# A convolution, Fourier-mix and MLP kernel on one core: another order of the opening, and a small norm product moved from VectorE to GpSimd

## The chip, the core and the metric

The kernel runs on one core of a Trainium2 chip. The core has five engines that run at the same time, each working through its own list of instructions in order: TensorE (matrix products; PE in the profile, with its weight loads listed apart as PEld), VectorE (DVE), ScalarE (ACT), GpSimd (POOL) and SyncE (SP), which here only starts DMA transfers. An instruction starts when those ahead of it on its engine have started or ended and the semaphores that it waits for are set. The metric is the device time of one execution in microseconds (us).

## The reference

Input `x` has 8 batches of 4224 positions and 192 features; `weight_gen` gives 8 heads x 7 taps for every position.

```python
w = exp(weight_gen - max(weight_gen, -1)); w = w / (sum(w, -1) + 1e-9)      # softmax over the 7 taps
x = einsum('bshk,bskhg->bshg', w, x_unf)        # causal 7-tap convolution; each head's taps act on its 24 features
u = x + real(fft(fft(x, axis=1), axis=2))       # mix over positions and over features
un = (u - mean(u)) / sqrt(var(u) + 1e-6)        # norm over the 192 features
out = u + maximum(un @ w_ch1, 0) @ w_ch2        # MLP 192 -> 768 -> 192
```

## The kernel before, in words

**Layout.** The 4224 positions of a batch lie as 128 partitions x 33 rows; the first Fourier transform is split into a 128-point and a 33-point part. Everything past the convolution works in nine groups of a batch: eight of four rows and a ninth of one row (suffix `_8`). So a tile name such as `ph_0_3` belongs to batch 0, group 3.

**Stages of one batch.** `conv` makes the taps (`softmax_taps`, lines 271 to 278: load, max, subtract, exp on ACT, sum, reciprocal) and then, for nine chunks of rows, seven products `u`/`pr` on DVE (line 390) that are added up by GpSimd (line 399). GpSimd then folds rows (`sm`, lines 411 and 413), TensorE does the 128-point transform (`pg`, line 418), ACT and DVE put it together (`gt`, lines 423 to 428), and SP writes it to device memory (`g_d`, lines 431 and 432) and reads it back in another layout (`g`, line 447). `transform` does the 33-point part (`pp`, line 457, copied to `pq` by ACT, line 461). `mix` does the transform over features for a group (`eo`, line 486) and adds it to `u` on DVE (lines 492 to 501). `norm` takes the mean and variance of a group: in the first groups ("quick": batch 0 groups 0 to 2, batch 1 groups 0 and 1) on DVE by its statistics instruction, elsewhere on ACT (`junk`, lines 522 and 526). It takes a square root on ACT and a reciprocal on DVE (line 529), then the bias product, mean x reciprocal, one DVE instruction for each of the four rows (line 531), then `un` on ACT (line 534), splits `un` into two fp16 halves (`hl`: line 538 on ACT, lines 540 and 542 on DVE for quick groups and on GpSimd elsewhere), and has a DMA transpose them to `ht` (line 545). `mlp` does six chunks of the first product (`ph`, line 570, five terms each), the relu (`hh`, line 576 alone on ACT; or line 580 on ACT and line 581 on DVE for the low half), the second product of the group before (`po`, line 597) and the closing sum (`u`, line 604), and the result is written out.

**Two forms of the second product.** For the first `F32_GROUPS` groups of batch 0, `po` is one fp32 product with the weights `w2f`, and the relu is one ACT instruction. From then on it is three fp16 terms (`w2h` and `w2l`), and the relu has the second instruction on DVE. The split of `w2f` into `w2h`/`w2l` (`split_w2`) is queued behind MLP group `SPLIT`. The weights come as 64-bit words and are turned into fp32 on DVE in the opening (`words_to_f32`, by `prep_w1` and `prep_w2`), with two scratch tiles in PSUM that share the three buffers of `ph`.

**What sets the order.** Each stage is a generator. `add(start, end, gen)` gives it a stretch of due times in units of one MLP group, and `run()` always advances the one that is due first. So conv of batch b+1, transform and mix of batch b, and the MLP of batch b-1 are woven into each other. The framework then orders every engine's list with its own model of times; `issue_after` (used by `behind` and `queue`) holds work back behind a named instruction: conv(2) behind the last `gt` of conv(1), later convs behind the last product of the one before. In the opening of batch 0 the mix and norm of groups 0 to 2 come first, with the conversion of the weights between them. All DMA transfers start from SP's list.

Of the kernel before, what the change touches and what calls it, by code (L numbers as in the profile page):

```python
# [31 lines left out]
HELD = 7.0  # L32
SPLIT = 5
PP_AT = 4.4
# [3 lines left out]
DVE_ADDS = {(1, c): 1 for c in range(1, NC)}  # L38
F32_GROUPS = 9

# [47 lines left out]
def tile_dynconv_fnet_mlp(  # L88
# [103 lines left out]

    def words_to_f32(raw, out, nm):

        hi, lo = raw[:, :, 1], raw[:, :, 0]
        v = nc.vector
        a, w = [pst("ph", 3, [P, PW], dt, f"{x}_{nm}") for x, dt in (("pa", I32), ("pw", F32))]
        t = temp(f"t_{nm}", I32)
        v.tensor_scalar(out=a, in0=hi, scalar1=3, scalar2=0x3FFFFFFF,
                        op0=ALU.logical_shift_left, op1=ALU.bitwise_and)  # L200
        v.scalar_tensor_tensor(out=t, in0=hi, scalar=-0x40000000, in1=a, op0=ALU.bitwise_and, op1=ALU.bitwise_or)
        v.tensor_scalar(out=a, in0=hi, scalar1=0x7FF00000, scalar2=None, op0=ALU.bitwise_and)
        v.scalar_tensor_tensor(out=w, in0=a, scalar=float(0x38100000), in1=t.bitcast(F32),
                               op0=ALU.is_ge, op1=ALU.mult)
        v.tensor_scalar(out=t, in0=w.bitcast(I32), scalar1=23, scalar2=23,
                        op0=ALU.logical_shift_right, op1=ALU.logical_shift_left)
        v.tensor_scalar(out=a, in0=lo, scalar1=3, scalar2=None, op0=ALU.logical_shift_right)
        r = t.bitcast(F32)
        v.scalar_tensor_tensor(out=r, in0=a, scalar=2.0 ** -49, in1=r, op0=ALU.mult, op1=ALU.mult)
        last_word.append(v.tensor_tensor(out=out, in0=w, in1=r, op=ALU.add))  # L210
# [21 lines left out]
    def prep_w1(raws):  # L232
# [3 lines left out]
        w = temp("w1f_1", F32)  # L236
        words_to_f32(raws[0], w, "w1_1")
        split_f32(w, hi, lo, s1)
# [4 lines left out]
        for i in range(2):  # L243
            cs_ = slice(i * PW, (i + 1) * PW)
            w = temp(f"w1f_0{i}", F32)
            words_to_f32(raws[1 + i], w, f"w1_0{i}")
            split_f32(w, w1h0[:, cs_], w1l0[:, cs_], s1)

    def prep_w2(i):
        words_to_f32(loaded[1][i], w2_part(i)[0], f"w2_{i}")  # L250

# [8 lines left out]
    def softmax_taps(b, parts):  # L260
# [7 lines left out]
        for lo, hi in parts:  # L268
# [5 lines left out]
                                    in1=m[:, sl].unsqueeze(2).broadcast_to([P, n, K]), op=ALU.subtract)  # L274
            nc.scalar.activation(w_sb[:, sl], w_sb[:, sl], AF.Exp)
            nc.vector.tensor_reduce(out=m[:, sl], in_=w_sb[:, sl], axis=AX.X, op=ALU.add)
            nc.vector.tensor_scalar_add(out=m[:, sl], in0=m[:, sl], scalar1=1e-9)
            nc.vector.reciprocal(out=m[:, sl], in_=m[:, sl])
            yield w_sb, m

    def mirrored(ap, step):
# [3 lines left out]
    def conv(b):  # L285

        g_d = g_ds[b % 2]
        parts = [(0, 5), (29, N2), (5, 29)] if b < 2 else [(0, N2)]
        taps = softmax_taps(b, parts)
        part_iter = iter(parts)  # L290
        pieces = iter(X_PIECES)
# [16 lines left out]
        def need_taps(c):  # L308
            nonlocal w_sb, ws
            while not rows_w.issuperset(rows_of(c)):  # L310
                rows_w.update(range(*next(part_iter)))
                w_sb, ws = next(taps)

# [12 lines left out]
        groups = [(NC, 0), (1, 2), (3, 4), (5, 6), (7,)] if b == 0 else [(c,) for c in range(NC + 1)]  # L326
        gt = None
        for grp in groups:
# [39 lines left out]
            for k in range(K):  # L368
                for c, R, u, wp, pa, wq, pt in chunks:
# [27 lines left out]
                    elif k > 0:  # L397
                        adder = nc.vector if k <= DVE_ADDS.get((b, c), 0) else nc.gpsimd
                        adder.tensor_tensor(out=u, in0=u, in1=pr, op=ALU.add)  # L399
                yield (done + sum(q[1] for q in chunks) * k / K) / N2  # L400
            for c, R, u, wp, pa, _, _ in chunks:
                if pa:
# [101 lines left out]
    def norm(b, g):  # L504
# [24 lines left out]
        nc.vector.reciprocal(out=rs[:, 0, 0:T], in_=rs[:, 0, 0:T])  # L529
        for t in range(T):  # L530
            nc.vector.tensor_scalar(out=rs[:, 1, t:t + 1], in0=st[:, t, 0:1], scalar1=rs[:, 0, t:t + 1],  # L531
                                    scalar2=neg, op0=ALU.mult, op1=ALU.mult)
        for t in range(T):
# [104 lines left out]
    def next_conv(b):  # L638
        yield from behind((last_gt if b == 2 else last_product)[b - 1].ins, conv(b))

# [14 lines left out]
    for at in behind(last_fold[0].ins, behind(lp, conv1)):  # L655
        if at > EARLY / N2:
            break
    queue(lp, (prep_w1, loaded[0]))
    for g in range(QUICK):
        add(0.0, 1.0, behind((last_word if g else last_split)[-1].ins, mix(0, g)))  # L660
        run()
        add(0.0, 1.0, norm(0, g))
        run()
        queue(last_bn[0, g].ins, (prep_w2, g))
    for i in range(QUICK, NH // 2):
# [5 lines left out]
    def late_split():  # L671
        yield 0.0
        with tc.issue_after(last_ph[SPLIT].ins):
            queue(last_product[1].ins, (split_w2, None))
        yield 1.0

    def held_mlp(n):
# [11 lines left out]
    for b in range(B):  # L689
# [6 lines left out]
        for g in range(NG):  # L696
            if b > 0 or g >= QUICK:
                at = t0 - mix_at + step * g
                add(at, at + step, mix(b, g))
                add(max(at + step, t0 + g - 2.0), t0 + g - 1.0, norm(b, g))  # L700
# [38 lines left out]
```

## Time and profile before

| what | value |
|---|---|
| runs | median 1191.4 us of 3 (1191.09 to 1192.69) |
| the profiled execution | 1194.52 us, of which its span from the first to the last instruction is 1192.7 us |
| TensorE busy, with weight loads apart | 1095.0 us (92% of the span) |
| VectorE busy | 1027.1 us (86%) |
| GpSimd busy | 867.8 us (73%) |
| ScalarE busy | 779.2 us (65%) |
| mean granted TensorE clock | 0.963 |

Times in the traces count from the start of the span. A row of a timeline gives the start, the duration, engine, line and operation, output and inputs, the number of merged instructions, and in brackets the idle time of that engine just before, with what ended it. A row of the windows gives each engine's busy time in a stretch, and the granted clock of TensorE as a share of full speed. A row of a group of instructions gives its total busy time, the mean duration of one in ns and the idle time before it. Durations in a group overlap by some 0.1 us where an engine is pipelined, so the pace of back-to-back instructions is a little quicker than their mean.

### The profile page before, as it was taken

The numbers are of one execution on the slowest core, as the hardware profiler recorded it, in microseconds if no ns is written. First come the engines' busy times: TensorE is split into PE (matmuls) and PEld (weight loads), VectorE is DVE, ScalarE is ACT, GpSimd is POOL, SyncE is SP. The second block draws the span as 40 slices with busy tenths as digits, with TensorE's granted clock in tenths as the row PEclk, the third lists the DMA queues.
The fourth block names the chain that finished last, engine by engine and source line by source line (L and its number), as shares of the span: only waits on it lengthen the run. The fifth ranks groups of instructions, "written<-read, shape, count | busy, mean of one in ns | idle before, by whom it ended". The sixth has DMA issues, their size and how long they took to land. (4 is left out here: it accounts for less than half of the span.)

```text
span 1192.7 us, 23723 instructions
## 1 busy us (share of the span) xinstructions
PE 1095.0 (92%) x8382; PEld 827.0 (69%) x8382; DVE 1027.1 (86%) x2041; ACT 779.2 (65%) x2353; POOL 867.8 (73%) x686
## 2 busy tenths in 40 slices
PE   4775599899899979998999999899989999999998
PEld 2444377678667857687677777678667876877677
DVE  7999998789999999899999999799998997367533
ACT  1015695254597598757895789657885799589732
POOL 3869579839896999699978999599958997002100
PEclk9896599999999989999999999899999999999999
DMA  8235233731348144733474247413543124412311
GB/s 305 84 98 163 40 60 109 192 89 47 99 127 206 50 123 102 191 87 88 112 198 110 61 114 208 125 48 110 147 121 92 54 58 102 111 45 71 75 50 44
DMA packets 156504, 128.73 MB, mean 108 GB/s; under 512 B 108571, under 2 KB 133088, under 8 KB 156384
## 3 DMA queue, kind: packets, MB, share of 16 engines
q1 hardware_dynamic: 156384, 127.21, 39.4%
q8 instruction: 66, 1.08, 0.4%
q14 instruction: 54, 0.44, 0.1%
HBM read 61.46 MB, written 39.37 MB: 85 GB/s over the span
## 5 line engine op out<-in xcount | busy, mean ns | idle before, releaser
L399 POOL TENSOR_TENSOR u<-u,pr 128x768 f32<-128x768 f32 (+1 forms) x395 | 655.3, 1679 | 69.5 <-DVE pr L390 62.6
L570 PE MATMUL ph<-ht,w1h 128*128 128x512 f16 (+1 forms) x1296 | 401.2, 366 | 20.1 <-DMA ht<-hl 8.8
L597 PE MATMUL po<-w2h,hh 128*128 128x192 f16 x2772 | 395.1, 247 | 6.4 <-DVE u L604 6.0
L597 PEld LDWEIGHTS <-hh 128*128 128x128 f16 x4158 | 355.0, 98 | 65.6 <-issue 7.8
L390 DVE TENSOR_TENSOR pr<-x_sb,wp 128x768 f32<-128x768 f32 (+1 forms) x420 | 358.0, 878 | 21.3 <-POOL u L399 16.8
L597 PE MATMUL po<-w2l,hh 128*128 128x192 f16 x1386 | 337.1, 247 | 0.0
L581 DVE SCALAR_TENSOR_TENSOR hh<-ph,hh 128x512 f16<-128x512 f32 (+1 forms) x378 | 238.7, 640 | 98.1 <-ACT hh L580 96.8
L570 PE MATMUL ph<-ht,w1l 128*128 128x512 f16 (+1 forms) x864 | 312.6, 365 | 0.0
L580 ACT ACTIVATE hh<-ph 128x512 f16<-128x512 f32 (+1 forms) x378 | 207.8, 555 | 136.6 <-PE ph L570 135.7
L540 POOL TENSOR_TENSOR hl<-un,hl 128x512 f16<-128x512 f32 (+1 forms) x67 | 71.9, 1073 | 175.3 <-ACT hl L538 129.4
L570 PEld LDWEIGHTS <-w1h 128*128 128x128 f16 x1296 | 127.2, 100 | 101.6 <-issue 6.1
L534 ACT ACTIVATE un<-u,rs 128x192 f32<-128x192 f32 x264 | 125.6, 537 | 19.8 <-DVE rs L531 12.2
L570 PEld LDWEIGHTS <-w1l 128*128 128x128 f16 x864 | 85.3, 99 | 73.2 <-issue 22.1
L526 ACT ACTIVATE junk<-u,rs 128x192 f16<-128x192 f32 x244 | 110.4, 453 | 3.5
L522 ACT ACTIVATE junk<-u 128x192 f16<-128x192 f32 x244 | 87.8, 360 | 16.6 <-DVE u L496 12.1
L486 PE MATMUL eo<-cs_sb,pq 97*128 97x97 f32 x544 | 79.8, 282 | 17.8 <-DVE u L496 13.3
L486 PEld LDWEIGHTS eo<-cs_sb,pq 97*128 97x128 f32 x544 | 73.8, 198 | 24.4 <-issue 13.1
L461 ACT COPY pq<-pp 97x204 f32<-97x204 f32 (+1 forms) x96 | 46.4, 483 | 60.3 <-PE pp L457 59.4
L597 PE MATMUL po<-w2f,hh 128*128 128x192 f32 x396 | 74.3, 337 | 3.5 <-DVE u L604 3.5
L597 PEld LDWEIGHTS po<-w2f,hh 128*128 128x128 f32 x396 | 68.3, 197 | 9.2 <-DVE u L604 5.2
L604 DVE SCALAR_TENSOR_TENSOR u<-po,isc,u 128x384 f32<-128x384 f32 (+1 forms) x119 | 68.0, 597 | 7.7 <-PE po L597 7.2
L395 PE MATMUL pa<-pr,ident 128*128 128x384 f32 x140 | 54.6, 540 | 20.5 <-DVE pr L390 17.8
(101 smaller groups left out, 1309.7 us busy)
## 6 DMA issues: line engine op xcount, KB each, us to landing
out_dram<-u SPq DMA_DIRECT2D x64, 384.0 KB
x_sb<-in_x_dram SPq DMA_DIRECT2D x48, 384.0 KB
g<-g_d SPq DMA_DIRECT2D x40, 336.0 KB
x_sb<-in_x_dram SPq DMA_DIRECT2D x8, 864.0 KB
g_d<-gt SPq DMA_DIRECT2D x32, 195.0 KB
g_d<-gt SPq DMA_DIRECT2D x32, 189.0 KB
w<-in_weight_gen_dram SPq DMA_DIRECT2D x6, 924.0 KB
x_sb<-in_x_dram SPq DMA_DIRECT2D x8, 672.0 KB
```

What stands on the lines that cost most here:

```text
L390: last_product[b] = nc.vector.tensor_tensor(out=dst, in0=rows, in1=wk, op=ALU.mult)
L399: adder.tensor_tensor(out=u, in0=u, in1=pr, op=ALU.add)
L486: nc.tensor.matmul(eo[:, e, j, :], lhsT=pq[0:DH, e, r, r:r + P], rhs=cs_sb[:, e, :], start=True, stop=True)
L522: nc.scalar.activation(junk, uv[:, t, :], AF.Identity, accum_out=st[:, t, 0:1])
L526: nc.scalar.activation(junk, uv[:, t, :], AF.Square, bias=rs[:, 2, t:t + 1], accum_out=st[:, t, 1:2])
L534: nc.scalar.activation(un[:, t, :], uv[:, t, :], AF.Identity, bias=rs[:, 1, t:t + 1], scale=rs[:, 0, t:t + 1])
L540: lo_eng.tensor_tensor(out=hl[:, 0:T, 2 * P:3 * P], in0=un[:, 0:T, 0:P], in1=hl[:, 0:T, 0:P], op=ALU.subtract)
L570: last_ph[n] = nc.tensor.matmul(ph[:, 0:T], lhsT=wt[:, cs_], rhs=ht[:, 0:T, blk], start=(i == 0), stop=(i == len(terms) - 1))
L580: nc.scalar.activation(a[:, 0:T], ph[:, 0:T], AF.Relu)
L581: nc.vector.scalar_tensor_tensor(out=l[:, 0:T], in0=ph[:, 0:T], scalar=0.0, in1=a[:, 0:T], op0=ALU.max, op1=ALU.subtract)
L597: nc.tensor.matmul(po[jj][:, s, :], lhsT=hx[:, t], rhs=wx[:, c2, :], start=(c2 == 0 and i == 0), stop=(c2 == NH - 1 and i == nt - 1))
L604: nc.vector.scalar_tensor_tensor(out=lt, in0=po[jj][:, 0:m], scalar=scales[0][:, 1:2] if NG * lb + lg < F32_GROUPS else isc, in1=lt, op0=A ...
```

## The change

1. `SPLIT` goes from 5 to 4 and `F32_GROUPS` from 9 to 7: groups 7 and 8 of batch 0 take the three-term fp16 form.
2. The scratch tiles of `prep_w2` take the two buffers of `po` in place of the three of `ph`.
3. The third part of the taps of batch 1 (rows 5 to 28) is made in two steps: load, max, subtract and exp along with `prep_w1`; sum and reciprocal behind the statistics of group (0, 0).
4. In conv(1), what follows the products of chunk 0 (`sm`, `pg`, `gt`) is held back behind those of the next chunk.
5. In `norm`, outside batch 0 and the quick groups, the four DVE products of line 531 become one GpSimd product of 128x4, of values that exist already.
6. conv(2) is held behind the last product of conv(1) instead of its last `gt`.
7. Mix of batch 0 from group 3 on is held behind the first MLP group, and is due 0.7 later.

```diff
-SPLIT = 5
+SPLIT = 4
-F32_GROUPS = 9
+F32_GROUPS = 7
...
-    def words_to_f32(raw, out, nm):
+    def words_to_f32(raw, out, nm, bank):
...
-        a, w = [pst("ph", 3, [P, PW], dt, f"{x}_{nm}") for x, dt in (("pa", I32), ("pw", F32))]
+        a, w = [pst(*bank, [P, PW], dt, f"{x}_{nm}") for x, dt in (("pa", I32), ("pw", F32))]
...
-        words_to_f32(loaded[1][i], w2_part(i)[0], f"w2_{i}")
+        words_to_f32(loaded[1][i], w2_part(i)[0], f"w2_{i}", ("po", 2))
...
             nc.scalar.activation(w_sb[:, sl], w_sb[:, sl], AF.Exp)
+            yield None
             nc.vector.tensor_reduce(out=m[:, sl], in_=w_sb[:, sl], axis=AX.X, op=ALU.add)
...
+    taps = {}
+
+    def tap_step(b, n):
+
+        t = taps[b]
+        while t["n"] < n:
+            t["n"] += 1
+            t["tiles"] = next(t["gen"]) or t["tiles"]
...
-            for c, R, u, wp, pa, _, _ in chunks:
+            tails += chunks
+            while tails and not (b == 1 and grp[0] == 0):
+                c, R, u, wp, pa, _, _ = tails.pop(0)
...
-        for t in range(T):
-            nc.vector.tensor_scalar(out=rs[:, 1, t:t + 1], in0=st[:, t, 0:1], scalar1=rs[:, 0, t:t + 1],
-                                    scalar2=neg, op0=ALU.mult, op1=ALU.mult)
+        if quick or b == 0:
+            for t in range(T):
+                nc.vector.tensor_scalar(out=rs[:, 1, t:t + 1], in0=st[:, t, 0:1], scalar1=rs[:, 0, t:t + 1],
+                                        scalar2=neg, op0=ALU.mult, op1=ALU.mult)
+        else:
+            nc.gpsimd.tensor_tensor(out=rs[:, 1, 0:T], in0=rs[:, 2, 0:T], in1=rs[:, 0, 0:T], op=ALU.mult)
...
-        yield from behind((last_gt if b == 2 else last_product)[b - 1].ins, conv(b))
+        yield from behind(last_product[b - 1].ins, conv(b))
...
     queue(lp, (prep_w1, loaded[0]))
+    queue(lp, (lambda n: tap_step(1, n), 5))
...
+        if g == 0:
+            queue(last_bn[0, 0].ins, (lambda n: tap_step(1, n), 6))
         queue(last_bn[0, g].ins, (prep_w2, g))
...
+    def late_mix(g):
+        yield from behind(last_ph[0].ins, mix(0, g))
...
-                at = t0 - mix_at + step * g
-                add(at, at + step, mix(b, g))
+                at = t0 - mix_at + step * g + (0.7 if b == 0 else 0)
+                add(at, at + step, late_mix(g) if b == 0 and g >= QUICK else mix(b, g))
```

Since the framework orders the lists anew, the diff does not show where things land. Three places follow. Line numbers of the kernel after are higher by 12 to 17 from `conv` on.

TensorE's list in the opening, before, from the mix products `eo` of batch 0 group 2 to the first MLP product `ph` (an `x4` joins four equal instructions):

```order
L486 MATMUL eo_2_874<-cs_sb,pq 128x97 x4
L486 MATMUL eo_3_925<-cs_sb,pq 128x97 x4
L486 MATMUL eo_4_948<-cs_sb,pq 128x97 x4
L418 MATMUL pg_0_666<-sm_0_663,f_sb 128x192 x2
L486 MATMUL eo_5_1022<-cs_sb,pq 128x97 x4
L570 LDWEIGHTS w1h_81
L570 MATMUL ph_0_0_936<-ht_0_810,w1h_81 128x512
```

The same place in the kernel after:

```order
L500 MATMUL eo_2_869<-cs_sb,pq 128x97 x4
L587 LDWEIGHTS w1h_81
L587 MATMUL ph_0_0_920<-ht_0_802,w1h_81 128x512
...
L500 MATMUL eo_3_930<-cs_sb,pq 128x97 x4
...
L500 MATMUL eo_4_979<-cs_sb,pq 128x97 x4
L432 MATMUL pg_1_1084<-sm_1_1081,f_sb 128x192 x2
```

The first MLP group now stands ahead of the mix of groups 3 and 4: fifteen of its products stand before `eo_3` and the other fifteen before `eo_4`.

GpSimd's list at the same time, from the last fold `sm` of batch 1's chunk 1 into chunk 2 (`u_2`), before:

```order
L411 TENSOR_TENSOR sm_1_1024<-u_1_677 128x2x191
L413 TENSOR_TENSOR sm_1_1024<-u_1_677 128x2
L540 TENSOR_TENSOR hl_3_1082<-un_3_1002,hl_3_1082 128x4x128
L542 TENSOR_TENSOR hl_3_1082<-un_3_1002,hl_3_1082 128x4x64
L540 TENSOR_TENSOR hl_4_1218<-un_4_1136,hl_4_1218 128x4x128
L542 TENSOR_TENSOR hl_4_1218<-un_4_1136,hl_4_1218 128x4x64
L399 TENSOR_TENSOR u_2_1191<-u_2_1191,pr_2_2_1206 128x768
```

And after:

```order
L425 TENSOR_TENSOR sm_1_1081<-u_1_665 128x2x191
L427 TENSOR_TENSOR sm_1_1081<-u_1_665 128x2
L411 TENSOR_TENSOR u_2_1180<-u_2_1180,pr_2_2_1195 128x768
L411 TENSOR_TENSOR u_2_1180<-u_2_1180,pr_2_3_1202 128x768
L411 TENSOR_TENSOR u_2_1180<-u_2_1180,pr_2_4_1223 128x768
L557 TENSOR_TENSOR hl_3_1065<-un_3_989,hl_3_1065 128x4x128
L559 TENSOR_TENSOR hl_3_1065<-un_3_989,hl_3_1065 128x4x64
```

The halves `hl` of batch 0's groups 3 and 4 stood ahead of the first add of chunk 2; now three adds go first, and group 4 comes six rows later still.

VectorE's list from the last product of conv(1) to the first of conv(2), with tile numbers, before:

```order
L390 TENSOR_TENSOR pr_1_8_6_1878<-x_sb_66,wp_1_623 128x192
...
L176 TENSOR_REDUCE mx_w2_1779<-ex_w20_1780 128x1
...
L428 TENSOR_TENSOR gt_1_8_1884<-pg_1_8_1882,up_1_8_1886 128x95
L272 TENSOR_REDUCE wp_2_1900<-w_2_1901 128x264
L182 TENSOR_REDUCE m2_w2_1791<-mr_w2_1792 1x1
L273 TENSOR_TENSOR w_2_1901<-w_2_1901,wp_2_1900 128x1848
...
L390 TENSOR_TENSOR u_2_0_1912<-x_sb_66,wp_2_1900 128x768
```

And after:

```order
L176 TENSOR_REDUCE mx_w2_1627<-ex_w20_1628 128x1
...
L402 TENSOR_TENSOR pr_1_8_6_1878<-x_sb_66,wp_1_623 128x192
...
L272 TENSOR_REDUCE wp_2_1900<-w_2_1901 128x264
...
L273 TENSOR_TENSOR w_2_1901<-w_2_1901,wp_2_1900 128x1848
...
L442 TENSOR_TENSOR gt_1_8_1884<-pg_1_8_1882,up_1_8_1886 128x95
L361 TENSOR_TENSOR wp_2_1900<-w_2_1901,wp_2_1900 128x224
L402 TENSOR_TENSOR u_2_0_1912<-x_sb_66,wp_2_1900 128x768
```

The maxima for the weight split (`mx_w2`) went ahead of the end of conv(1), and the taps of conv(2) (`wp_2`, `w_2`) no longer stand behind the last `gt` of conv(1).

More of the change, by code (lines that the diff above doesn't have):

```diff
@@ L236, in prep_w1 @@
         w = temp("w1f_1", F32)
-        words_to_f32(raws[0], w, "w1_1")
+        words_to_f32(raws[0], w, "w1_1", ("ph", 3))
         split_f32(w, hi, lo, s1)
@@ L245, in prep_w1 @@
             w = temp(f"w1f_0{i}", F32)
-            words_to_f32(raws[1 + i], w, f"w1_0{i}")
+            words_to_f32(raws[1 + i], w, f"w1_0{i}", ("ph", 3))
             split_f32(w, w1h0[:, cs_], w1l0[:, cs_], s1)
     def prep_w2(i):
-        words_to_f32(loaded[1][i], w2_part(i)[0], f"w2_{i}")
+        words_to_f32(loaded[1][i], w2_part(i)[0], f"w2_{i}", ("po", 2))
     def split_w2(_):
@@ L288, in conv @@
         parts = [(0, 5), (29, N2), (5, 29)] if b < 2 else [(0, N2)]
-        taps = softmax_taps(b, parts)
-        part_iter = iter(parts)
+        taps[b] = dict(gen=softmax_taps(b, parts), n=0, tiles=None)
+        part_iter = iter(range(len(parts)))
         pieces = iter(X_PIECES)
@@ L310, in need_taps @@
             while not rows_w.issuperset(rows_of(c)):
-                rows_w.update(range(*next(part_iter)))
-                w_sb, ws = next(taps)
+                i = next(part_iter)
+                rows_w.update(range(*parts[i]))
+                tap_step(b, 2 * i + 2)
+                w_sb, ws = taps[b]["tiles"]
         if b > 0:
@@ L326, in conv @@
         groups = [(NC, 0), (1, 2), (3, 4), (5, 6), (7,)] if b == 0 else [(c,) for c in range(NC + 1)]
-        gt = None
+        gt, tails = None, []
         for grp in groups:
@@ L399, in conv @@
                         adder.tensor_tensor(out=u, in0=u, in1=pr, op=ALU.add)
-                yield (done + sum(q[1] for q in chunks) * k / K) / N2
-            for c, R, u, wp, pa, _, _ in chunks:
+                yield (done + sum(q[1] for q in tails) + sum(q[1] for q in chunks) * k / K) / N2
+            tails += chunks
+            while tails and not (b == 1 and grp[0] == 0):
+                c, R, u, wp, pa, _, _ = tails.pop(0)
                 if pa:
```

## The prediction

> **What bounds the kernel now.** The totals come first:
>
> ```profile
> PE 1095.0 (92%) x8382; PEld 827.0 (69%) x8382; DVE 1027.1 (86%) x2041; ACT 779.2 (65%) x2353; POOL 867.8 (73%) x686
> ```
>
> TensorE is the busiest engine, but 92% is a mean over stages. The chain of waits says what the end hung on:
>
> ```profile
> 888.85 2.80 DMA g_d<-gt
> 891.79 3.57 DMA g<-g_d
> 895.50 2.40 PE pp L457 x16
> ...
> 1188.14 1.66 PE po L597 x18
> ```
>
> The end hangs on `pp` of batch 6 at 895.50, and that on the round trip of `gt` through memory behind conv(6). Next come the windows, each from the first product of one conv to that of the next, conv(1)'s chunk 2 first. The columns are the length, then the busy time of PE, PEld, DVE, ACT and POOL, then PE's clock, DMA share and GB/s:
>
> ```profile
> 152.80:255.40 102.60, 97.26 (x532) 74.52 (x530) 84.22 (x143) 54.10 (x148) 76.46 (x60) 0.97 0.49 126
> 255.40:381.10 125.70, 117.58 (x873) 88.92 (x873) 120.92 (x243) 86.15 (x257) 110.75 (x84) 1.00 0.41 106
> 381.10:506.80 125.70, 116.85 (x972) 88.48 (x971) 120.23 (x242) 96.83 (x300) 112.55 (x88) 0.97 0.45 122
> 506.80:631.90 125.10, 119.77 (x1017) 92.34 (x1015) 118.81 (x240) 95.89 (x299) 112.72 (x88) 0.99 0.46 120
> 631.90:757.80 125.90, 123.60 (x1039) 95.49 (x1038) 121.20 (x244) 98.52 (x303) 113.01 (x88) 0.99 0.44 120
> 757.80:887.40 129.60, 122.96 (x1025) 94.16 (x1023) 121.68 (x244) 96.41 (x298) 110.45 (x84) 0.97 0.41 111
> 887.40:1021.10 133.70, 130.58 (x1090) 100.25 (x1088) 117.07 (x243) 99.01 (x307) 115.16 (x92) 0.99 0.34 87
> 1021.10:1192.70 171.60, 168.14 (x1478) 129.27 (x1476) 83.49 (x186) 102.77 (x308) 14.98 (x18) 1.00 0.23 61
> ```
>
> From 887 on TensorE idles 133.70 - 130.58 + 171.60 - 168.14 = 6.6 us in 305: it alone is the bound. In the five windows from 255.4 to 887.4 DVE idles 4.8, 5.5, 6.3, 4.7 and 7.9 us (29.2 together), TensorE 8.1, 8.9, 5.3, 2.3 and 6.6 (31.2), GpSimd 13 to 19: DVE and TensorE are nearly tied, GpSimd close behind. In the first window nothing but TensorE is full (DVE 82%, POOL 75%), so conv(1) and what follows it take longer than their work. A shift there is handed on from conv to conv, as far as TensorE keeps up.
>
> **The change part by part.** *Before conv(1)'s chunk 2.* Its products came behind the third part of the taps, and GpSimd's adds behind the `hl` of groups 3 and 4:
>
> ```profile
> 142.22 1.55 DVE L272 TENSOR_REDUCE wp<-w 128x192 f32<-128x1344 f32 x1
> ...
> 149.00 1.56 DVE L276 TENSOR_REDUCE wp<-w 128x192 f32<-128x1344 f32 x1 [1.85 <-ACT w L275]
> ...
> 152.82 0.95 DVE L390 TENSOR_TENSOR u<-x_sb,wp 128x768 f32<-128x768 f32 x1
> ```
> ```profile
> 153.30 1.16 POOL L540 TENSOR_TENSOR hl<-un,hl 128x512 f16<-128x512 f32 x1 [16.41 <-ACT hl L538]
> ...
> 159.43 1.16 POOL L540 TENSOR_TENSOR hl<-un,hl 128x512 f16<-128x512 f32 x1 [4.34 <-ACT hl L538]
> ...
> 161.17 5.60 POOL L399 TENSOR_TENSOR u<-u,pr 128x768 f32<-128x768 f32 x3
> ```
>
> The DVE work of the taps is not saved, it moves ahead; the wait of 1.85 us goes, and part of the mix and norm of groups 3 to 5 now falls behind the products. I take -5 us for the first product (bounds -2, the wait alone, and -10.6, all from 142.22 to 152.82). The first add no longer waits for both `hl` (8.35 us behind the first product until now). With five products and one DVE add ahead of it I take it 7 us earlier, at 154.2. From there GpSimd has to work off the adds of conv(1); the two `hl` pairs, some 1.8 us each (159.43 to 161.17), now lie among these, which gives back 3.6. So conv(1) ends some 3.5 us earlier, between 0 and 7.
>
> *From conv(1) to conv(2).*
>
> ```profile
> 229.07 0.35 DVE L390 TENSOR_TENSOR pr<-x_sb,wp 128x192 f32<-128x192 f32 x1 [0.20 <-POOL u L399]
> ...
> 229.87 4.17 DVE L175 TENSOR_SCALAR ex_w<-w2f 128x384 int32<-128x384 int32 x3
> ...
> 242.08 0.26 DVE L427 TENSOR_TENSOR gt<-pg,up 128x95 f32<-128x95 f32 x1 [5.03 <-ACT up L425]
> ...
> 255.39 0.95 DVE L390 TENSOR_TENSOR u<-x_sb,wp 128x768 f32<-128x768 f32 x1
> ```
> ```profile
> 365.59 0.34 DVE L390 TENSOR_TENSOR pr<-x_sb,wp 128x192 f32<-128x192 f32 x1
> ...
> 381.08 0.95 DVE L390 TENSOR_TENSOR u<-x_sb,wp 128x768 f32<-128x768 f32 x1
> ```
>
> From the last product of one conv to the first of the next it is 255.39 - 229.07 = 26.3 us here, and 381.08 - 365.59 = 15.5 one batch on, where the taps don't stand behind the last `gt`. The new list makes this transition like the later ones, and the 4.17 us for the weight split moves into conv(1), where DVE idles 18 us. I take 15 for the 26.3, so -11.5 (bounds -5, the wait of 5.03 alone, and -14). Conv(2) starts 3.5 + 11.5 = **15 us earlier**, at 240.4 (bounds 5 and 21, both ends together).
>
> *Norm's bias product.*
>
> ```profile
> 145.68 0.57 DVE L531 TENSOR_SCALAR rs<-st,rs 128x1 f32<-128x1 f32 x4
> ```
> ```profile
> L531 DVE TENSOR_SCALAR rs<-st,rs 128x1 f32<-128x1 f32 x264 | 38.2, 205 | 0.5
> L581 DVE SCALAR_TENSOR_TENSOR hh<-ph,hh 128x512 f16<-128x512 f32 x336 | 227.5, 684 | 91.1 <-ACT hh L580 89.9
> ```
> ```profile
> L413 POOL TENSOR_TENSOR sm<-u 128x2 f32<-128x2 f32 x64 | 14.8, 231 | 0.0
> ```
>
> Four take 0.57 us. Of 264, batch 0 and batch 1's two quick groups keep 33 + 8 = 41, so 223 go: 33 a batch, 33 x 0.57 / 4 = 4.7 us. GpSimd gets nine products a batch. None like it is in the trace; between the 128x2 fold (0.23) and a pair `hl` (1.8), it is nearest to the fold, so 9 x 0.23 = 2.1 us a batch. If DVE set the pace, each of the five windows would shorten by 4.7; if GpSimd did, it would lengthen by 2.1. Neither does alone: GpSimd adds behind DVE's products within a chunk, DVE sets the transitions, and TensorE idles only 2.3 us in the fourth window.
>
> ```profile
> POOL u L399 <- DVE pr L390: 46.3, 12, 22.8
> ```
> ```profile
> DVE pr L390 <- POOL u L399: 5.8, 11, 1.5
> ```
>
> These waits from 255 to 888 show both directions; without the 22.8 of the first start, GpSimd waits 23.5 us for DVE. I take 0 for the product in the five windows (bounds -4.7 and +2.1 each).
>
> *The fp16 form of groups 7 and 8.*
>
> ```profile
> 170.76 4.17 PE L597 MATMUL po<-w2f,hh 128*128 128x192 f32 x24 [1.45 <-DVE u L604]
> ```
> ```profile
> 1112.84 0.99 PE po L597 x12
> ```
>
> A group of four rows takes 48 fp32 products at 4.17 / 24 = 0.174 us, 8.3 us, or 72 in fp16 at 0.99 / 12 = 0.083, 5.9 us: 2.4 less for group 7, a quarter of it for group 8, 3 us of TensorE. On DVE it adds 6 relu halves of 0.684 and 6 shorter ones, some 5.5 us, and the order puts those of group 7 into conv(2)'s chunk 2. DVE idles 4.8 us in that window, so half is hidden: **+2.5 us** (bounds 0 and 5.5; without cover 5.5).
>
> *TensorE's order.* With the first MLP group ahead of the mix of groups 3 and 4, TensorE has work sooner, but that group runs against ACT, which makes its relus and the norm of group 3; the order of what follows is as before, and I take 0 for TensorE's idle time up to 150 (bounds -4 and +4). Counting the products of the new list at their durations, `pp` of batch 2 has 15.8 us less work ahead of it and that of batch 6 2.2 less, so TensorE has 13.6 us more to do in between.
>
> ```profile
> 383.10 0.91 PE L457 MATMUL pp<-te_sb,g 102*97 102x102 f32 x8 [1.17 <-DMA g<-g_d]
> ```
>
> From 383.10 to 895.50, about the last four of the five windows, it idles 8.9 + 5.3 + 2.3 + 6.6 = 23.1 us. With both `pp` 12.5 us earlier it would have 9.5 left, 2.4 a window, as little as the fourth window has now (2.3): just enough. No term, but a bound for what follows. Behind `pp` of batch 6 there are 290 us of its work in both lists: 0.
>
> **Sum:** -15 + 0 + 2.5 + 0 = -12.5 us. The profiled execution took 1194.52, 3.1 over the median of the runs, so 1182.0 for it, and **1179** for the median.
>
> A row that speaks of a price beside this:
>
> ```profile
> 141.89 0.42 DVE L542 TENSOR_TENSOR hl<-un,hl 128x256 f16<-128x256 f32 x1
> ```
> ```profile
> L542 DVE TENSOR_TENSOR hl<-un,hl 128x256 f16<-128x256 f32 x5 | 7.7, 1542 | 0.0
> ```
>
> The same instruction on DVE took 0.42 us where GpSimd was idle, and 1.54 on average. The Trainium skill, "GPSIMD Engine Reference", section "8. Key points", says that GpSimd shares its SBUF interfaces with VectorE and contends with instructions that have two SBUF inputs; by it, 2.1 us more of GpSimd in a batch cost DVE at most 2.1 x (1 - 0.42 / 1.54) = 1.5 us (an estimate), five times 7.5, if DVE did nothing but such instructions, and the sum would be -5 instead of -12.5. The trace agrees on the direction, but the convolution's product on DVE, the commonest, reads its taps from PSUM.
>
> **The rivals.** *DVE sets the pace, the gain grows.* For it: DVE idles less than TensorE in the first two of the five windows. `pp` of batch 2 would come 15 - 2.5 + 4.7 = 17.2 us earlier. Against it: TensorE has only 23.1 - 13.6 = 9.5 us of idle time to give up from there on, and will keep one a window: 17.2 + 5.5 = 22.7, 1169; with the opening at its bound of 21, 1163.
>
> *GpSimd sets the pace.* Its adds hardly pause within a chunk, and five windows times 2.1 give back 10.5: -15 + 10.5 = -4.5, 1187. Against it: it idles 13 to 19 us in each window.
>
> *TensorE doesn't use the earlier conv(2).* It is busy for 97.26 of 102.60 us in the first window already, and the 13.6 us more behind `pp` of batch 2 may cost it what conv gains; then only the 3 us of saved products remain: 1188.5, at the edge of no change. Against it: that idle time is in part waiting for this very chain, as the 1.17 us at 383.10.
>
> *Slower: GpSimd waits at the new product.* It works in order. The product waits for DVE's reciprocal, and that for ACT's square root; the adds behind it wait too, and DVE's products for their buffers. The price is the wait, up to 1.8 us for the reciprocal where DVE itself waited:
>
> ```profile
> DVE rs L529 <- ACT rs L528: 8.1, 8, 1.8
> ```
>
> Over the 45 products of the five windows it decides from (15 - 10.5 + 2.4) / 45 = 0.15 us each; at 0.4 it is -4.5 + 18 = +13.5, 1205. For it: the old products stood on the engine that also makes the reciprocal, the new one crosses to another. Against it: 8.1 us in 8 waits is little in a whole run.
>
> **How the numbers follow.** A difference under 0.2%, 2.4 us, can't be told from none here. Chances: the forecast, between -20 and -8, 0.50; DVE 0.09; GpSimd 0.17; TensorE 0.13, half of it within 0.2%; slower 0.11. That is 0.825 faster, 0.065 the same, 0.11 slower. The range is 1164 to 1191: below, nearly to the end of DVE's case; above, past GpSimd's and TensorE's, short of the slower one.
>
> **What would show it.** Right: conv(2)'s first product near 240 and `pp` of batch 2 near 371; windows of 125 to 129 us after that; `pp` of batch 6 near 883, and 297 us from there to the end. The wait of 16.41 for `hl` ahead of GpSimd's adds is gone, and the new product takes under 0.3 us. Wrong at the opening: conv(2) starts after 250. Wrong at the product: GpSimd shows a wait for the reciprocal of more than 7 us in all, or adds pause behind it. Wrong on the hand-over: conv(2) is early and `pp` of batch 6 is not; then either DVE's or TensorE's idle time in the windows tells which took it.

## The result, and the profile after

The kernel after takes **1174.94 us** (median of 4 runs, 1171.40 to 1176.11) against 1191.87 for the kernel before in the same session, 16.9 us less by the medians. The ratio of the runs is 0.9845, 95% interval 0.9815 to 0.9874, which makes 18 us, and the two spans that are compared below differ by 18.4. The forecast was 1179, 12.5 us less, in a range of 1164 to 1191. Direction and range were right; the size was a quarter to a third too small, and the experiments show that some of the reasons behind it were wrong.

The totals and TensorE's clock from the page of the kernel after (span 1174.3 us):

```profile
PE 1087.7 (93%) x8412; PEld 823.8 (70%) x8412; DVE 1007.1 (86%) x1830; ACT 774.0 (66%) x2351; POOL 874.7 (74%) x747
```

TensorE is idle 1174.3 - 1087.7 = 86.6 us instead of 97.7. The windows of the kernel after, cut at the same places as before (from conv(1)'s chunk 2, then from the first product of one conv to that of the next; columns: length, busy PE, PEld, DVE, ACT, POOL, PE's clock, DMA share, GB/s):

```profile
145.80:240.90 95.10, 91.58 (x504) 71.38 (x504) 84.86 (x160) 56.48 (x166) 75.40 (x60) 0.98 0.43 120
240.90:369.20 128.30, 116.63 (x862) 88.83 (x861) 120.84 (x224) 86.84 (x260) 111.34 (x91) 0.93 0.42 114
369.20:494.00 124.80, 122.72 (x1043) 94.83 (x1041) 118.77 (x211) 98.68 (x304) 114.07 (x98) 1.00 0.48 123
494.00:619.90 125.90, 123.86 (x1040) 95.15 (x1038) 118.45 (x212) 97.95 (x301) 113.93 (x97) 0.99 0.48 124
619.90:745.90 126.00, 123.51 (x1038) 95.38 (x1037) 117.71 (x211) 97.66 (x302) 114.00 (x97) 0.99 0.45 120
745.90:874.80 128.90, 124.28 (x1058) 95.61 (x1057) 119.12 (x214) 98.07 (x303) 113.84 (x97) 1.00 0.47 117
874.80:1174.30 299.50, 293.82 (x2548) 225.88 (x2546) 190.91 (x360) 198.30 (x610) 130.68 (x124) 1.00 0.28 71
```

And the last stretch of the kernel before, cut in the same way:

```profile
887.40:1192.70 305.30, 298.72 (x2567) 229.52 (x2564) 200.56 (x429) 201.78 (x615) 130.14 (x110) 0.99 0.28 72
```

Conv(2) starts 14.5 us earlier (255.4 to 240.9) and conv(3) 11.9 (381.1 to 369.2). The next four windows add up to 505.6, where they were 506.3. The last stretch, in which TensorE has hardly a pause, is 5.8 us shorter, mostly because TensorE has 293.82 us left to do there instead of 298.72: with windows as long as before it got more done in them (494.4 us busy against 483.2 from conv(3) to conv(7)). So the 18.4 us of the two spans are 11.9 up to conv(3) and 6.5 behind it. TensorE's clock is lower in one window: from conv(2) to conv(3) it was granted 0.93 of full speed, in the kernel before 1.00.

How the opening came about, on VectorE and then on GpSimd (timeline of the kernel after):

```profile
145.79 0.95 DVE L402 TENSOR_TENSOR u<-x_sb,wp 128x768 f32<-128x768 f32 x1
...
226.53 0.34 DVE L402 TENSOR_TENSOR pr<-x_sb,wp 128x192 f32<-128x192 f32 x1
...
227.39 2.08 DVE L272 TENSOR_REDUCE wp<-w 128x264 f32<-128x1848 f32 x1
...
240.94 0.95 DVE L402 TENSOR_TENSOR u<-x_sb,wp 128x768 f32<-128x768 f32 x1
```
```profile
152.34 5.63 POOL L411 TENSOR_TENSOR u<-u,pr 128x768 f32<-128x768 f32 x3 [18.35 <-DVE u L411]
157.93 1.16 POOL L557 TENSOR_TENSOR hl<-un,hl 128x512 f16<-128x512 f32 x1
```

The products of chunk 2 start 7.0 us earlier (152.8 to 145.8), the adds 8.9 (161.2 to 152.3) and without the wait for `hl`; conv(1)'s last product comes 2.5 us earlier (229.1 to 226.5), and the way from there to conv(2) takes 14.4 us instead of 26.3.

### The profile page after: what moved, and what is told of

Same layout as the page of the kernel before. It is cut to its first block, busy times and chain, and to the rows that moved or that the text cites. A ratio compares the mean times of both kernels' runs of the same rounds, so it can differ in the third digit from the quotient of the medians.

```text
span 1174.3 us, 23548 instructions
## 1 busy us (share of the span) xinstructions
PE 1087.7 (93%) x8412; PEld 823.8 (70%) x8412; DVE 1007.1 (86%) x1830; ACT 774.0 (66%) x2351; POOL 874.7 (74%) x747
## 4 chain that ended last, share of the span: by engine, by line
PE 31%; ACT 9%; POOL 7%; issue 6%; DVE 3%; DMA 3%; SPq 0%; POOLq 0%; DVEq 0%; ACTq 0%
PE po L614 13%; PE ph L587 13%; POOL u L411 5%; PE pp L471 3%; ACT un L551 2%; ACT hh L597 2%; DMA g<-g_d 2%; ACT junk L540 2%; PE eo L500 1%; ACT junk L536 1%; DMA g_d<-gt 1%; POOL hl L557 1%; PE pg L432 1%; ACT hl L555 1%; DVE pr L402 1%
## 5 line engine op out<-in xcount | busy, mean ns | idle before, releaser
L614 PE MATMUL po<-w2h,hh 128*128 128x192 f16 x2832 | 408.2, 248 | 8.0 <-DVE hh L598 6.9
L614 PEld LDWEIGHTS <-hh 128*128 128x128 f16 x4248 | 364.7, 99 | 67.4 <-DVE hh L598 7.5
L614 PE MATMUL po<-w2l,hh 128*128 128x192 f16 x1416 | 345.6, 248 | 0.0
L598 DVE SCALAR_TENSOR_TENSOR hh<-ph,hh 128x512 f16<-128x512 f32 (+1 forms) x390 | 244.1, 633 | 112.5 <-ACT hh L597 111.5
L597 ACT ACTIVATE hh<-ph 128x512 f16<-128x512 f32 (+1 forms) x390 | 212.7, 550 | 147.5 <-PE ph L587 146.4
L425 POOL TENSOR_TENSOR sm<-u 128x382 f32<-128x382 f32 x64 | 64.5, 1008 | 7.0 <-ACT u L420 6.8
L614 PE MATMUL po<-w2f,hh 128*128 128x192 f32 x336 | 63.9, 334 | 3.0 <-DVE u L621 3.0
```

The lines of the kernel that those rows point to most:

```text
L597: nc.scalar.activation(a[:, 0:T], ph[:, 0:T], AF.Relu)
L598: nc.vector.scalar_tensor_tensor(out=l[:, 0:T], in0=ph[:, 0:T], scalar=0.0, in1=a[:, 0:T], op0=ALU.max, op1=ALU.subtract)
L614: nc.tensor.matmul(po[jj][:, s, :], lhsT=hx[:, t], rhs=wx[:, c2, :], start=(c2 == 0 and i == 0), stop=(c2 == NH - 1 and i == nt - 1))
```

## The experiments

Every kernel was timed against the kernel before on the same chip. The table has the ratio with its interval, and from the one profiled execution the start of conv(2) and of conv(3), and the time from there to the end of the span.

| kernel | ratio (95% interval) | conv(2) | conv(3) | conv(3) to end |
|---|---|---|---|---|
| before | 1 | 255.4 | 381.1 | 811.6 |
| after | 0.9845 (0.9815 to 0.9874) | 240.9 | 369.2 | 805.1 |
| u_product: after, product on VectorE | 0.9928 (0.9908 to 0.9948) | 241.7 | 371.1 | 814.0 |
| o_product: before, product on GpSimd | 0.9963 (0.9947 to 0.9979) | 254.1 | 381.9 | 803.9 |
| u_last_gt: conv(2) behind the last `gt` | 0.9916 (0.9903 to 0.9930) | 251.2 | 375.8 | 807.1 |
| u_f32: SPLIT 5, F32_GROUPS 9 | 0.9943 (0.9923 to 0.9963) | 239.2 | 379.8 | 803.7 |
| s4_f9: SPLIT 4, F32_GROUPS 9 | 0.9896 (0.9868 to 0.9923) | 241.6 | 375.4 | 805.0 |
| u_taps: taps in one step | 0.9936 (0.9915 to 0.9957) | 245.7 | 381.9 | 804.9 |
| u_mix: mix not held back | 0.9920 (0.9899 to 0.9940) | 247.9 | 383.3 | 807.2 |
| u_bank_tails: scratch in `ph`, tail not held | 0.9901 (0.9882 to 0.9921) | 245.8 | 373.9 | 807.1 |
| x_product0: product on GpSimd in batch 0 too | 0.9892 (0.9863 to 0.9922) | 245.2 | 374.4 | 807.9 |
| s3_f6: SPLIT 3, F32_GROUPS 6 | 0.9926 (0.9909 to 0.9942) | 242.9 | 375.7 | 808.3 |
| l_term: less TensorE work | 0.9827 (0.9812 to 0.9842) | 241.0 | 371.4 | 801.1 |
| d_product: product made four times | 1.0172 (1.0151 to 1.0194) | 241.0 | 369.3 | 842.9 |

The profiled execution of u_mix took 7 us more than the median of its runs and that of u_taps 4 more, the others were within 3.1 of theirs. Executions of one kernel differ by up to 12 us (x_product0: 1174.99 to 1187.35), so a difference of a few us between two rows is not firm. The last two kernels do other work behind conv(3). Of the other twelve, the ten with the product on GpSimd take 803.7 to 808.3 us from conv(3) to the end and the two with it on VectorE 811.6 and 814.0, whatever the opening did. So in these executions nearly every difference between them is made in two places: at the start of conv(3), and by the product.

### The product, there and back

u_product:

```diff
-        if quick or b == 0:
+        if True:
```

> The kernel after with the bias product back on VectorE (four small products a group instead of one on GpSimd). Theory (the gain is made in the opening, and from conv(3) to conv(6) TensorE sets the pace, so the product moves nothing there): within 3 us of the kernel after, 1172 to 1178, conv(2) still starting near 241. Rival (VectorE's relief of 4.7 us a batch is what shortened conv(6) and conv(7), where some 6 us more were gained than forecast): 1179 to 1183, conv(7) taking 110 us from its first to its last product instead of 105.8. Third (the product on GpSimd costs, since it waits for the reciprocal): 1165 to 1171.

o_product is the kernel before with the `else` branch of the change in `norm` and nothing else.

> The kernel before with nothing but the bias product moved to GpSimd. Theory: no change beyond 3 us, 1188 to 1195. Rival (VectorE's relief counts): 1180 to 1187. Third (GpSimd sets the pace, 2 us a batch and waits for the reciprocal): 1196 to 1206.

The theory fell in both, in the second narrowly. u_product's 1185.9 lies above its rival's band of 1179 to 1183 too; by the ratio it would be 1183.3. Taken back, the product costs 0.9928 / 0.9845, some 10 us; put into the kernel before it saves 0.37%, 4.4 us. The windows of u_product from conv(3) on:

```profile
371.10:497.40 126.30, 123.50 (x1045) 94.86 (x1045) 121.20 (x244) 97.96 (x305) 115.22 (x92) 1.00 0.46 122
497.40:621.50 124.10, 119.84 (x1017) 92.61 (x1018) 120.71 (x244) 96.40 (x300) 112.75 (x88) 1.00 0.44 119
621.50:747.50 126.00, 121.15 (x1036) 93.54 (x1034) 120.80 (x243) 98.24 (x300) 112.20 (x86) 1.00 0.47 120
747.50:878.50 131.00, 125.39 (x1026) 95.89 (x1025) 121.32 (x245) 97.42 (x300) 111.02 (x86) 0.96 0.44 118
878.50:1185.10 306.60, 301.26 (x2601) 231.02 (x2599) 202.40 (x431) 201.34 (x617) 130.07 (x110) 1.00 0.28 70
```

Up to conv(7), conv runs at nearly the same pace as in the kernel after (507.4 us against 505.6). Conv(7) itself takes 108.9 us from its first product to the end of its last, where the kernel after takes 105.9 and the rival had said 110; but the ten kernels with the product on GpSimd lie between 105.8 and 108.6 there, so this sign separates little. Behind its last product another 4.1 us are lost (197.8 against 193.7). So the rival had a part of it right, and most of the loss lies behind the start of conv(7). VectorE is busy 2.2 to 3.1 us longer in each window, and TensorE gets 489.9 us done in the four windows instead of 494.4; the stretch from conv(7) on is 7.1 us longer and holds 7.4 us more of TensorE's work. That the MLP falls behind because its relus stand in VectorE's fuller list fits this; the runs don't separate it from other ways.

The product itself, in the kernel after:

```profile
L549 POOL TENSOR_TENSOR rs<-rs 128x4 f32<-128x4 f32 x54 | 10.9, 206 | 64.3 <-DVE rs L543 60.4 <-ACT junk L540 3.9
```

### More of GpSimd, less of TensorE

d_product makes the same product four times; the output does not change:

```diff
-            nc.gpsimd.tensor_tensor(out=rs[:, 1, 0:T], in0=rs[:, 2, 0:T], in1=rs[:, 0, 0:T], op=ALU.mult)
+            for _ in range(4):
+                nc.gpsimd.tensor_tensor(out=rs[:, 1, 0:T], in0=rs[:, 2, 0:T], in1=rs[:, 0, 0:T], op=ALU.mult)
```

> The kernel after with the product on GpSimd made four times instead of once, 0.6 us more of GpSimd a group and 5.4 a batch, with the same output. Theory (GpSimd has slack in the windows, 114 of 125 us): from conv(3) to the end it stays at 804 to 809, ratio 0.984 to 0.989. Rival (within a conv GpSimd sets the pace, with 0.6 to 3 us of idle time there): about 5 us more a batch from conv(3) on, 825 to 830, ratio 1.002 to 1.010.

l_term leaves out one term of the first MLP product in batches 1 to 5, so its output is not the whole result:

```diff
-                terms = ((w1h0, 0), (w1l0, 0), (w1h0, 2), (w1h1, 1), (w1l1, 1))
+                terms = ((w1h0, 0), (w1l0, 0), (w1h0, 2), (w1h1, 1), (w1l1, 1))[:4 if 1 <= b <= 5 else 5]
```

> The kernel after with one of the five terms of the first MLP product (low weights on the last 64 features, w1l1) left out in batches 1 to 5, so that TensorE has some 6 x 0.216 = 1.3 us less to do in a group, 11 in a batch, 53 in all; the other engines do the same work. So far the time from conv(3)'s first product to the end was 804 to 807 in seven kernels with the product on GpSimd and 812 to 814 in two with it on VectorE. Theory (behind conv(3) TensorE, with 17 us of idle time in 804, sets the end, VectorE next to it): the windows of 125 us from conv to conv shorten only to VectorE's work, 119 to 121, but the rest behind conv(7) gets shorter too: ratio 0.945 to 0.965, TensorE's idle time much larger. Rival (TensorE alone): 53 us less, ratio 0.938 to 0.942. Rival (the chain over VectorE and GpSimd sets the windows, and the end hangs on it): windows stay within 1 us of 125, ratio 0.970 to 0.983.

l_term speaks against TensorE as the bound of the windows. With some 42 us less to do (TensorE busy 1045.5 us in place of 1087.7), it is hardly faster than the kernel after: the intervals 0.9812 to 0.9842 and 0.9815 to 0.9874 overlap. Its ratio is at the slow end of the third case, and three of its windows (126.7, 125.9, 130.9 and 126.5 us) are longer than that case said, with TensorE idling 7 to 14 us in each. The four add up to 510.0 us, where the kernel after has 505.6. The first three:

```profile
371.40:498.10 126.70, 118.58 (x1041) 93.64 (x1039) 119.77 (x215) 97.47 (x304) 113.81 (x97) 1.00 0.48 127
498.10:624.00 125.90, 117.82 (x1022) 92.50 (x1021) 119.45 (x213) 98.44 (x305) 114.04 (x97) 0.99 0.46 122
624.00:754.90 130.90, 116.46 (x969) 92.50 (x968) 117.59 (x211) 97.01 (x301) 114.03 (x97) 0.93 0.45 120
```

In the third of them TensorE's clock was 0.93, and over the whole execution 0.954 against 0.965. From conv(7) on less work does show: the last stretch is 291.1 us instead of 299.5, for 15.0 us less of TensorE's work.

d_product is 3.3% slower than the kernel after, some 39 us, for 904.1 - 874.7 = 29.4 us of GpSimd's time. Its windows:

```profile
511.00:639.00 128.00, 122.90 (x1030) 93.56 (x1028) 117.93 (x208) 92.83 (x291) 115.50 (x119) 0.99 0.45 119
639.00:770.60 131.60, 128.78 (x1080) 99.22 (x1078) 118.82 (x213) 101.90 (x309) 117.77 (x124) 0.99 0.46 121
770.60:902.00 131.40, 122.47 (x1021) 94.02 (x1019) 119.25 (x210) 97.15 (x299) 118.00 (x124) 0.99 0.40 104
```

GpSimd has 1.6, 3.8 and 4.2 us more to do in them than in the kernel after, and they are 2.1, 5.6 and 2.5 us longer, in sum about one for one, though GpSimd still idles 12 to 14 us in each. But this does not show that GpSimd sets the pace. The framework did not keep the four products of a group together. In one group of conv(2) the first starts at 318.01 and the fourth at 328.21, and `un`, which reads them, comes behind the fourth; in the kernel after that group's one product is at 317.78 and its `un` at 321.55. So the norm is late by more than the products take:

```profile
318.01 0.20 POOL L550 TENSOR_TENSOR rs<-rs 128x4 f32<-128x4 f32 x1
...
328.21 0.20 POOL L550 TENSOR_TENSOR rs<-rs 128x4 f32<-128x4 f32 x1
329.48 1.85 ACT L552 ACTIVATE un<-u,rs 128x192 f32<-128x192 f32 x4
```

And the window before them (conv(3), 141.7 us) is 16.9 longer, of which GpSimd's own work explains 3.3. There the list of VectorE's waits does not name GpSimd; it waited 15.9 us for the relu on ACT, in the kernel after 0.8. A row of waits gives the total in us, how often, and the longest (this window in d_product, then in the kernel after):

```profile
DVE hh L599 <- ACT hh L598: 15.9, 13, 4.5
```
```profile
DVE hh L598 <- ACT hh L597: 0.8, 3, 0.3
```

The relu in turn waited for TensorE's products, and TensorE had a late start: at 375.39 it had waited 4.66 us for `g`, and the eight products that took 0.91 us in the kernel after (370.64) took 1.65, at a granted clock of 0.62 from 370 to 382:

```profile
375.39 1.65 PE L471 MATMUL pp<-te_sb,g 102*97 102x102 f32 x8 [4.66 <-DMA g<-g_d]
```

What the two show together is less than a bound: TensorE's work does not set the pace of 125 us, and more work for GpSimd in the middle of the norm costs more than its own time. Whether that is GpSimd's share or the later norm, and what then sets the pace, was not settled; each of the two kernels also has a list of its own.

### The opening, part by part

```diff
-        yield from behind(last_product[b - 1].ins, conv(b))
+        yield from behind((last_gt if b == 2 else last_product)[b - 1].ins, conv(b))
```

> The kernel after with conv(2) held behind the last gt of conv(1) again. Theory (the way from conv(1) to conv(2) is worth some 11 us of the 15 at conv(2)'s start, and is handed on to the end): conv(2) starts 5 to 11 us later, at 246 to 252, and the time is 1180 to 1186. Rival (a later start is made up in the next batches by TensorE's idle time): conv(2) later by as much, the time within 3 us of the kernel after.

Here the theory held: conv(2) starts 10.3 us later, and the ratio of 0.9916 against 0.9845 is 8.5 us more.

```diff
-SPLIT = 4
+SPLIT = 5
-F32_GROUPS = 7
+F32_GROUPS = 9
```

> The kernel after with SPLIT 5 and F32_GROUPS 9 again. Theory: 3 us more of TensorE's work, 5.5 less of VectorE's in the first window, and the weight split falls behind conv(1) again (some 5 us of VectorE at the transition): conv(2) starts 3 to 6 us later, the time is 1176 to 1181. Rival (the fp16 form costs VectorE more than it saves TensorE): 1168 to 1173.

s4_f9 has only the second of the two lines.

> The kernel after with F32_GROUPS 9 again but SPLIT left at 4: the two changes of u_f32 taken apart. Theory A (u_f32 lost because the split of the weights fell into the start of conv(2), where VectorE then waited 6.28 us for a product that stands far back on TensorE): the split stays inside conv(1), so only the 3 us of TensorE's work come back: ratio to before 0.985 to 0.989. Theory B (the fp32 form of groups 7 and 8 is what cost): 0.992 to 0.996, as u_f32.

Neither expectation was met, s4_f9's theory A by a hair (0.9896, said up to 0.989). u_f32 starts conv(2) no later but earlier, at 239.2, and loses it all in the window that follows, 140.6 us in place of 128.3, in good part because the split of the weights now stands among the products of conv(2). VectorE's timeline there:

```profile
252.86 0.16 DVE L185 TENSOR_SCALAR m_w<-me_w 128x1 f32<-128x1 f32 x1 [6.28 <-PE me_w L184]
```

A tiny instruction waits 6.28 us for TensorE, and the products behind it wait too. s4_f9 keeps the split inside conv(1) and gets back half (0.9943 to 0.9896). The other half, 0.9896 against 0.9845 or 6 us, is left to the fp32 form of groups 7 and 8, though the two intervals touch (0.9868 to 0.9923 and 0.9815 to 0.9874). Its window of conv(2) is 133.8 us, and TensorE's timeline there shows one long wait for a closing sum on VectorE:

```profile
285.80 7.20 PE L614 MATMUL po<-w2f,hh 128*128 128x192 f32 x26 [7.92 <-DVE u L621]
```

The 26 products behind it take 0.277 us each where 24 of the same took 0.174 in the kernel before (170.76), at a clock of 0.67 from 277.7 to 293 instead of 1.00. So with F32_GROUPS at 7 this kernel is some 6 us faster, where the forecast had a cost of 2.5; how much of that is the form and how much the place of one wait in the list isn't separated.

u_taps takes out the two queued steps, so that the third part of the taps is made ahead of chunk 2 again; u_mix makes `late_mix` and the 0.7 void:

```diff
-    queue(lp, (lambda n: tap_step(1, n), 5))
...
-        if g == 0:
-            queue(last_bn[0, 0].ins, (lambda n: tap_step(1, n), 6))
```
```diff
-                at = t0 - mix_at + step * g + (0.7 if b == 0 else 0)
-                add(at, at + step, late_mix(g) if b == 0 and g >= QUICK else mix(b, g))
+                at = t0 - mix_at + step * g
+                add(at, at + step, mix(b, g))
```

> The kernel after with the third part of batch 1's taps again made right ahead of the products of conv(1)'s chunk 2. Theory: the first product of chunk 2 comes some 5 us later than in the kernel after (145.8), at 149 to 153, conv(2) by 2 to 5 later, ratio to before 0.987 to 0.991. Rival (VectorE works the same amount by then and the wait of 1.85 us is hidden anyway): within 2 us of the kernel after, 0.983 to 0.986.

> The kernel after with mix of batch 0 from group 3 on neither held behind the first MLP group nor due 0.7 later. Theory: the first MLP products fall behind the mix of groups 3 to 5 again and the mix takes VectorE ahead of conv(1)'s chunk 2: that starts 4 to 7 us later than at 145.8, ratio 0.988 to 0.993. Rival (the taps alone make the earlier start): within 2 us, 0.983 to 0.986.

The start of chunk 2 came as expected, at 151.6 and 150.4, and conv(2) 4.8 and 7.0 us later. u_mix met its expectation with 0.9920; u_taps lost 11 us, more than the expected band. Both then wait in the window of conv(2) for the relu of an MLP group that isn't far enough (VectorE's timeline of u_taps, then of u_mix):

```profile
266.53 0.69 DVE L598 SCALAR_TENSOR_TENSOR hh<-ph,hh 128x512 f16<-128x512 f32 x1 [6.70 <-ACT hh L597]
```
```profile
268.02 0.69 DVE L598 SCALAR_TENSOR_TENSOR hh<-ph,hh 128x512 f16<-128x512 f32 x1 [4.28 <-ACT hh L597]
```

u_bank_tails:

```diff
-        words_to_f32(loaded[1][i], w2_part(i)[0], f"w2_{i}", ("po", 2))
+        words_to_f32(loaded[1][i], w2_part(i)[0], f"w2_{i}", ("ph", 3))
...
-            while tails and not (b == 1 and grp[0] == 0):
+            while tails:
```

> The kernel after with the scratch tiles of prep_w2 in the three buffers of ph again, and the tail of conv(1)'s chunk 0 not held back. Theory: the first MLP group waits for a scratch tile again, as before (4.1 us at its third chunk), while the end is set later: ratio 0.985 to 0.988. Rival (TensorE's idle time counts in full wherever it lies): 0.988 to 0.991.

It came out in the rival's band, 0.9901, 7 us slower, but conv(2) also started 4.9 us later, so this is no proof of the rival. Both edits show as waits of TensorE in the opening: 15.09 us for the fold of conv(1) ahead of `pg` at 128.15, and 6.05 and 5.54 us for VectorE's work on the weights ahead of the first MLP products at 135.86 and 143.69. Which of the two sets the later conv(2) was not tried.

The six undos cost 10, 8.5, 12, 11, 9 and 7 us, 57 together, three times what the change brings. They are not parts of a sum: each gets its own list, and a part that loses a few us at conv(2) can meet a wait behind it that the full change does not have. A rival stands untested here: the kernel after may have a list that happens to fit, so that any edit costs some us whatever it does. All nine edits of it that keep the whole computation and its work (the six undos, s4_f9 and the two below) are slower, by 6 to 12 us, in whichever direction they go, and no edit that should change nothing was run beside them. The product stands on firmer ground, since it also gained 4.4 us in the kernel before.

### Further in the same direction

x_product0 drops `or b == 0` from the condition in `norm`; s3_f6 has SPLIT 3 and F32_GROUPS 6.

> The kernel after with the product on GpSimd in batch 0's groups 3 to 8 too, 21 small VectorE products less in the opening, 3 us. Theory (the opening hangs on VectorE up to conv(2), and what conv(3) gains is handed on): ratio 0.981 to 0.984. Rival (GpSimd is the fuller engine in conv(1), the product waits there for the reciprocal): 0.986 to 0.992.

> The kernel after with SPLIT 3 and F32_GROUPS 6, one step further in the direction of the change: the split of the weights is queued a group earlier and group 6 takes the fp16 form, 2.4 us less of TensorE, 4.1 more of VectorE. Theory (conv(2) starts where it does, and TensorE's saving shows at conv(3)): ratio 0.981 to 0.985. Rival (VectorE's extra work in the opening costs as much or more): 0.986 to 0.990.

Both are slower than the kernel after, by 6 and 10 us, x_product0 within its rival's band (its interval touches that of the kernel after), s3_f6 beyond its own. In x_product0 GpSimd waits at the first of the new products, between the start of conv(1)'s chunk 2 at 146.8 and conv(2)'s at 245.2 (waits of GpSimd there):

```profile
POOL rs L549 <- DVE rs L543: 17.5, 1, 17.5
POOL u L411 <- DVE pr L402: 1.5, 2, 0.9
```

This wait takes the place of one that GpSimd had there anyway (18.35 us at 152.34, above). What is late is the end of conv(1), whose last product ends at 231.4 instead of 226.9; the split's chain waits 3.9 us for TensorE in the middle of it, 2.4 in the kernel after. No kernel tried here that does the whole computation beats the kernel after.

## Why the prediction was right or wrong, point by point

- **The opening, right.** "Conv(2) starts 15 us earlier, at 240.4": it starts at 240.9. Its two steps came out at 2.5 (said 3.5) and 11.9 (said 11.5). That the way to conv(2) would be like the later ones was the most useful comparison; u_last_gt, which undoes it, starts conv(2) 10.3 us later and ends 8.5 later.
- **The first window, right in size and wrong in its reason.** +2.5 was forecast, +2.6 measured, and `pp` of batch 2 at 370.64 (said 371). But the step laid it to the fp16 form of groups 7 and 8, and in s4_f9, with that form undone, the window is 5.5 us longer, not 2.5 shorter. The step compared the work that is added to VectorE with VectorE's idle time in that window, and left out TensorE, whose clock there was 0.93 instead of 1.00 and which waits 3.95 us in one place for a relu half (309.74). What made the 2.6 isn't shown, so its match with 2.5 is luck.
- **The product, the step that failed.** "I take 0 for the product in the five windows": the windows are indeed the same, but behind conv(3) 6.5 us were gained, and u_product against the kernel after gives 8.9 in the same stretch (814.0 to 805.1), over the five windows 1.3 to 1.8 us each, within the stated bounds of -4.7 and +2.1. The step looked only at the length of the windows. What TensorE gets done in windows of equal length is paid out from conv(7) on.
- **"Behind `pp` of batch 6: 0", wrong by 2.2 us.** `pp` of batch 6 came at 879.25, 16.2 us earlier (said 12.5), and from there to the end it took 2.2 us less. The 290 us counted from the lists were the same in both, and TensorE's busy time is not: it is 7.3 us less in the whole execution, where 3 were counted. The rest was not traced.
- **TensorE as the bound of the windows, wrong.** The forecast had it "just enough", with 2.4 us of idle time a window, and measured were 2.1, 2.0, 2.5 and 4.6. The number was right, but l_term shows that it does not bound the windows: with less work it idles more, and the four add up to 510.0 us instead of 505.6. From conv(7) on, where TensorE idles 5.7 us in 299.5, it does.
- **The rivals.** That GpSimd would set the pace is not borne out: the product on it pays, and d_product, which is slower, does not separate GpSimd's work from the later norm. The slower case, a wait at the product, is there in the waits of GpSimd from 240.9 to 874.8: 9.3 us in 5, over the 7 that were named as a sign. It did little harm as far as the rows show: 5.66 of it fall behind the last add of a conv, where GpSimd has nothing else to do:

```profile
482.23 0.62 POOL L411 TENSOR_TENSOR u<-u,pr 128x192 f32<-128x192 f32 x1
482.78 0.22 POOL L549 TENSOR_TENSOR rs<-rs 128x4 f32<-128x4 f32 x1
488.66 0.19 POOL L549 TENSOR_TENSOR rs<-rs 128x1 f32<-128x1 f32 x1 [5.66 <-DVE rs L543]
```

- **The shared SBUF interface.** The estimate by the Trainium skill's "GPSIMD Engine Reference", section "8. Key points", made the sum -5 us, and it was -18. VectorE's commonest instruction did not become slower (878 ns before, 876 after, over all forms), but it is the one that reads its taps from PSUM, and so no test of that sentence. No run here tested the contention by itself.

## What to carry to other kernels

Where two chains share the engines, a conv that is paced by its own chain and a products' backlog that is worked off at the end, a gain can appear in neither the pace nor the windows: compare how much the backlog's engine gets done in windows of equal length. An engine's idle time in a window says little about whether it is the bound: TensorE idled 2 to 5 us, and with 4 to 7 us less work for it in each the four windows together were 4.4 us longer. Added work is no clean test of room either: four products in place of one took GpSimd about 0.5 us more a group, and in one group the instruction behind them came 8 us later. And parts of a reordering are not to be priced one by one from undos, since each undo makes another list; an edit that should change nothing, run beside them, would tell how much another list costs by itself.

## What was not expected of the hardware

A GpSimd product of 128x4 took 206 ns, no more than the 128x2 fold (231 before, 209 after); three more of them in a group cost about 0.16 us each (29.4 us for 183). Four VectorE products of 128x1, 0.57 us, cost the kernel more than one GpSimd product in the two comparisons from batch 1 on (u_product and o_product); in batch 0's groups 3 to 8 (x_product0) the move to GpSimd did not pay.

TensorE ran slower for some us after each of three waits that were looked at: after 4.66 us (d_product) eight products took 1.65 us instead of 0.91, after 7.92 us (s4_f9) an fp32 product 0.277 instead of 0.174, and behind the 3.95 us at 309.74 in the kernel after the clock was 0.61 from 306 to 319. A wait of TensorE can cost more than its own length.
